# A transformer layer with compressive memory: copying projections out of PSUM in pairs, masks by two heads, tiles at a pitch of 130, another warm-up and another order

## The chip, the cores and the metric

The kernel runs on one core of one Trainium2 chip. The metric is the device time of one execution in microseconds (us). A core has five engines with a queue each: PE (TensorE, the matmuls; its weight loads are shown as PEld), DVE (VectorE), ACT (ScalarE), POOL (GpSimd) and SP (SyncE, which issues nearly all DMAs here). An engine takes its instructions in the order of its queue and stops at one whose semaphore has not come yet.

## The reference

The input x has 2048 rows of 576 columns. Everything is bfloat16 in memory.

```python
h  = x + attention(layernorm(x), wq, wk, wv, wo, beta)       # 32 heads of 18 columns
h2 = h + (gelu(layernorm(h) @ w1 + b1) @ w2 + b2)            # w1: 576 x 4608, w2: 4608 x 576

# attention, for each of 4 segments of 512 rows
p     = softmax(q_s @ k_s.T * 18**-0.5 + causal mask)
o     = g * (phi(q_s) @ M) / (phi(q_s) @ z + 1e-6) + (1 - g) * (p @ v_s)    # g = sigmoid(beta)
M, z  = M + phi(k_s).T @ v_s, z + sum(phi(k_s))              # phi(t) = t + 1 above 0, exp(t) below
```

For segment 0 the memory M is zero, so only the softmax part counts there; all later segments read a memory that the earlier ones have filled.

## The kernel before, in words

**The order is written out.** The kernel first builds a list of operations (`add`). Each has a tag of its stage, a name, a function that issues its instructions, the operations it comes behind (`after`), the buffers it acquires (`acq`) and uses. The table `TIMETABLE` gives each an engine and a slot: `"B00Po": "p 264"` puts that projection on PE in slot 264; the letters are p (PE), a (ACT), d (DVE), g (POOL) and s (SP). All operations are issued in the order of their slots, so this table is the order of every engine's queue. The costs that stand beside the operations choose which buffer of a set an operation gets; the order does not depend on them.

**Stages.** X is the first layernorm: of each tile of 128 rows DVE sums (`stats`, L752), POOL forms the reciprocal deviation (`rstd`, L769 and L770), and DVE writes the normalized tile `xn` in bfloat16 (`apply`, L782; L780 for the first two, which only subtract the mean, the deviation being put into the copies of the projections behind them). `xn` is then turned: for X0 and the first two tiles of X1 by PE transposes out of a tile with 640 columns in one run (`transposes`, L790, copied out of PSUM by `copy`), for the others through DRAM by a transposing DMA (`flip`, L665).

P projects q, k and v. `proj_pair` (L843) computes a tile's 576 output columns as two halves of 288, each in a PSUM bank of its own. It is two operations, P and R. If they stand next to each other in PE's queue they are issued as ten matmuls over 128 rows (L875); if another operation stands between them they are issued as 18 matmuls over 64 rows each (L849), and a small memset (`pass`, L855) on DVE or POOL lies between the two. Each half was copied out of PSUM by an operation of its own (`copy`, L669 to L680: ACT at L675, DVE at L679, with a factor L673 and L677) into `qk_pad` (q and k, 32 columns for each head) or `v_aug`. `qk_pad` goes to DRAM and comes back turned by flips; the flips of segment 1 are called `A1flip`. From k also come `pk` and `fk` (L955), which with v make the memory update M (L979, L991).

A0 is the attention of segment 0, in `step` (L1044): scores on PE (`st0`, L1060) for four heads at a time, two activations exp on ACT, each over 1024 columns of PSUM (L1009), then the causal mask on the blocks of the diagonal: one operation for all four heads and two blocks, 128 x 1024 (on DVE a product with a triangle, L1072; on POOL an affine select, L1075). It came behind both exponentials. Then values on PE (L1091), a 32x32 transposition on DVE (`valT`, L1105), reciprocals (`rec`, L1109 and L1110), the division (`comb`, L1114, DVE or POOL), a copy of two leftover columns per head (`swap`), and five transpositions on DVE per pair of row tiles into `oT` (L1130); those of the first pair are called `A01oT`. A1 to A3 do the same for the later segments, with the memory (scores L1220, masks L1232 and L1234, values L1245, memory L1191 and L1194).

B is the output projection, by the same `proj_pair` (so `B00Po` is the first half of that of segment 0's first tile), the residual and the second layernorm (`apply`, L782 again). C is the first matmul of the MLP (F1: L1394 for segment 0, L1357 for the others), copied out with b1 (L1405, L1372, L1370, L1362) and put through gelu (L1377, L1411). D is the second one (F2, L1446), with the residual (L1459).

**The start.** PE warms up on a tile `pt` that DVE first sets to zero (L683), in three operations of 4, 3 and 2 matmuls (L689). A gate (`gate_x`, L739) copies one element of x on DVE once x has landed; the DMAs of some weights and of more x are held until then (`held`, L727). The list `begin` holds back later fills and loads in the same manner: `ones`, two activations on ACT that set a column of `v_aug` to one, and on POOL the fills of the blocks of the memory (`memset`, `eps`, `gmz`).

Of the kernel before, what the change touches and what calls it, by code (L numbers as in the profile page):

```python
# [25 lines left out]
    "A00exp": "a 93 103 111 128",  # L26
    "A00mask": "g 162 132 182 179",
    "A00st0": "p 90 110",
    "A01comb": "d189 g198 d236 g240",
    "A01exp": "a 148 151 160 164 180 184 171 173",  # L30
    "A01mask": "g169 d158 g193 g194",
    "A01oT": "d 209 244 253 252 261",
    "A01rec": "d 177 192 226 224",
    "A01st0": "p 140 159 178 166",
    "A01swap": "g 256 251",
    "A01val": "p 172 218",
    "A01valT": "d 176 175 223 219",
    "A02comb": "g 407 430",
    "A02exp": "a 210 213 242 243 225 228 263 270 282 292 314 317 339 345",
    "A02mask": "g 238 260 298 362",  # L40
    "A02rec": "d 376 410",
    "A02st0": "p 197 234 216 258 280 304 335",
    "A02val": "p 302 303 371 372",
    "A02valT": "d 311 379",
    "A03comb": "g 483 498",
    "A03exp": "a 365 366 403 408 374 375 412 413 417 418 439 449 452 465",
    "A03mask": "g 414 388 423 470",
    "A03oT": "d 445 460 516 519 543",
    "A03rec": "d 442 493",
    "A03st0": "p 364 386 373 405 416 429 451",  # L50
    "A03swap": "g 525 532",
    "A03val": "p 434 438 489 490",
    "A03valT": "d 441 491",
    "A0flip": "s 89 86 141 117 183 188 259 348",
    "A1comb": "g622 g683 g750 g788 d834 g866 g905 g907",
    "A1comb2": "d641 g692 d772 g804 g847 d870 g935 d910",
    "A1eg": "a 436 428 617 702 548 768 746 817",
    "A1exp": "a 499 500 515 518 510 512 614 616 588 589 627 628 649 650 666 669 691 693 710 713 734 737 779 781 754 756 801 806 810 815 790 792 848 859 "
        "869 874 877 882 831 832",
    "A1flip": "s 421 420 572 631 478 695 662 807",  # L60
    "A1mask": "g554 d546 g556 g559 g542 g644 g621 g600 d655 g667 g694 g703 g718 g730 g742 d749 d755 g791 d793 d796 g819 g814 g844 g822 g794 d872 g862 g891 "
        "g880 g894 g890 g856",
    "A1mem": "p 530 454 682 761 709 849 811 878",
    "A1memT": "d 531 455 688 773 719 851 813 879",
    "A1memfin": "g607 g533 g766 g789 g777 g861 d919 g900",
    "A1oT": "d 823 873 871 936 937",
    "A1pq": "d 511 440 677 748 698 836 799 867",
    "A1rec": "d 561 464 745 780 765 852 840 881",
    "A1rec2": "d 599 663 733 775 828 858 902 904",
    "A1rg": "g 501 425 584 696 604 743 770 830",  # L70
    "A1st": "p 494 514 509 606 586 624 647 665 679 704 726 764 740 800 805 787 843 854 876 825",
    "A1swap": "d911 g920",
    "A1val": "p 590 648 708 763 808 846 892 895",
    "A1valT": "d 591 653 712 774 816 853 898 901",
    "A2comb": "d1034 d1078 g1154 g1120 g1166 d1192 g1289 g1275",
    "A2comb2": "g1070 d1081 d1222 g1145 d1167 g1217 g1292 d1283",
    "A2eg": "a 889 930 1097 1058 1012 1136 1171 1210",
    "A2exp": "a 917 918 893 896 924 925 908 914 940 942 1032 1044 1045 1051 1027 1030 1064 1068 1073 1074 1104 1106 1092 1100 1126 1129 1112 1117 1132 "
        "1137 1159 1160 1176 1178 1227 1234 1184 1188 1202 1204",
    "A2flip": "s 786 845 916 984 969 1080 928 1182",  # L80
    "A2mask": "d985 g1006 d987 d977 g965 g956 g962 g966 d1057 d1076 g1079 d1047 g1052 g1077 g1089 d1088 g1115 d1107 d1118 d1139 g1142 g1158 g1170 d1162 "
        "g1211 d1228 g1220 d1241 g1235 g1206 d1209 d1225",
    "A2mem": "p 931 1009 1147 1084 1127 1177 1239 1240",
    "A2memT": "d 941 1028 1148 1095 1140 1185 1247 1246",
    "A2memfin": "g976 g1053 d1216 g1122 d1163 d1195 g1274 g1269",
    "A2oT": "d 1111 1264 1244 1299 1303",
    "A2pq": "d 906 979 1099 1067 1024 1153 1197 1226",
    "A2rec": "d 975 1042 1190 1121 1150 1191 1254 1266",
    "A2rec2": "d 1023 1066 1119 1113 1157 1186 1265 1271",
    "A2rg": "g 860 951 1046 1060 1005 1133 1172 1189",  # L90
    "A2st": "p 915 888 923 903 939 1031 1040 1007 1056 1069 1101 1083 1124 1109 1130 1144 1165 1223 1183 1201",
    "A2swap": "g 1297 1293",
    "A2val": "p 1014 1013 1085 1090 1146 1179 1243 1242",
    "A2valT": "d 1017 1018 1093 1096 1149 1180 1255 1250",
    "A3comb": "g1389 g1417 g1468 d1513 d1563 g1585 g1653 d1633",
    "A3comb2": "d1431 g1432 g1523 d1548 d1645 g1594 g1662 d1636",
    "A3eg": "a 1280 1298 1394 1388 1516 1478 1550 1564",
    "A3exp": "a 1272 1273 1281 1288 1290 1296 1390 1391 1306 1307 1436 1437 1409 1415 1398 1399 1445 1450 1426 1428 1518 1526 1462 1466 1480 1481 1528 "
        "1531 1501 1504 1557 1560 1593 1603 1605 1607 1567 1569 1576 1577",
    "A3flip": "s 1238 1214 1302 1286 1333 1439 1421 1458",  # L100
    "A3mask": "d1309 g1304 d1329 g1338 g1359 d1396 g1347 d1314 d1446 d1418 d1425 g1444 g1435 d1454 d1449 g1443 d1532 g1472 g1474 g1537 g1514 d1536 g1509 "
        "g1525 d1590 g1626 g1604 d1608 g1621 g1572 d1588 d1602",
    "A3mem": "p 1381 1352 1471 1463 1541 1533 1616 1617",
    "A3memT": "d 1387 1353 1494 1491 1553 1534 1644 1618",
    "A3memfin": "g1419 g1393 d1496 g1510 d1638 d1551 g1660 g1631",
    "A3oT": "d 1498 1624 1659 1665 1667",
    "A3pq": "d 1313 1342 1401 1448 1527 1493 1582 1584",
    "A3rec": "d 1412 1368 1495 1497 1580 1535 1654 1623",
    "A3rec2": "d 1357 1416 1464 1507 1562 1559 1646 1630",
    "A3rg": "g 1301 1215 1375 1354 1512 1490 1482 1545",  # L110
    "A3st": "p 1262 1278 1287 1380 1305 1429 1406 1397 1442 1413 1508 1457 1477 1524 1500 1543 1589 1601 1561 1573",
    "A3swap": "a1661 g1656",
    "A3val": "p 1346 1402 1459 1465 1546 1544 1628 1627",
    "A3valT": "d 1348 1414 1461 1469 1549 1547 1641 1629",
    "B00Po": "p 264",
    "B00Ro": "p 272",
    "B00T": "p 336 340",
    "B00apply": "d 315",
    "B00copy": "d 338 341",
    "B00dma": "s 232 540",  # L120
    "B00hadd": "d 279 281",
    "B00pass": "d 266",
    "B00rstd": "g 312",
    "B00stats": "d 309",
    "B00tail": "g 326",
    "B01Po": "p 274",
    "B01Ro": "p 278",
    "B01T": "p 343 346",
    "B01apply": "d 325",
    "B01copy": "d 344 347",  # L130
    "B01dma": "s 235 447",
    "B01hadd": "d 283 294",
    "B01pass": "d 275",
# [12 lines left out]
    "B03Po": "p 610",
    "B03Ro": "p 612",
    "B03apply": "d 656",
    "B03dma": "s 549 769 678",
    "B03flip": "s 776 778",  # L150
    "B03hadd": "d 613 615",
    "B03pass": "d 611",
    "B03rstd": "g 654",
    "B03stats": "d 635",
    "B03tail": "d 660",
    "B1Po": "p 944 959 961 947",
    "B1Ro": "p 949 970 971 950",
# [345 lines left out]
def kernel(  # L503
# [12 lines left out]
    P = 128  # L516
# [1092 lines left out]
```

## Time and profile before

| | us |
|---|---|
| median of 3 runs | 442.07 (442.07 to 442.28) |
| the profiled execution | 442.22 |
| its span, first to last instruction | 440.5 |
| PE busy | 431.3 of it (98%), 5152 matmuls |
| DVE, ACT, POOL busy | 289.6, 300.0, 179.7 |
| moved by DMA | 75.61 MB |

The profile is one execution. A row of a group reads: line, engine, operation, written tile <- read tile with partitions x elements, count | busy us, mean ns of one | idle time of the engine just ahead of them, and the releaser that ended most of it. A row of the chain or of the timeline reads: start in us from the span's start, length, then engine, tile and line, and in brackets the idle time ahead of it. A row of a window reads: stretch, length, busy us (and instructions) of PE, PEld, DVE, ACT and POOL, the granted TensorE clock, the mean share of the DMA engines and GB/s. The granted clock was 1.000 of full speed in the whole span.

### The profile page before, as it was taken

Reading aid. Unit: us, or ns where it says so; the run is one execution under the profiler, and the core shown is the slowest. Engines: PE = TensorE matmul, PEld = TensorE weight load, DVE = VectorE, ACT = ScalarE, POOL = GpSimd, SP = SyncE. Lnnn points to the kernel's source line nnn. Section 1 sums busy time; section 2 is a strip of 40 time slices with the busy share of each in tenths; the row PEclk is TensorE's granted clock in tenths of the full one; section 3 lists DMA queues with packets and bytes.
Section 4 is the critical chain, followed back from the end, with each engine's and each line's share of the span. In section 5 each row is a group of like instructions: output and inputs, shape, how many; then the busy total and the mean of one; then the engine's idle time right before and its main releaser. Section 6 shows DMA issues by size and latency. Waiting matters only on the chain.

```text
span 440.5 us, 12357 instructions
## 1 busy us (share of the span) xinstructions
PE 431.3 (98%) x5152; PEld 278.7 (63%) x5152; DVE 289.6 (66%) x650; ACT 300.0 (68%) x344; POOL 179.7 (41%) x327
## 2 busy tenths in 40 slices
PE   8997999999999999999999999999999999999997
PEld 4764677766677676663445766644457775446885
DVE  5899999998889869749797877784957101000111
ACT  5998789999988888786989966556974001755000
POOL 4698676757557454445223643512304100000001
PEclk9999999999999999999999999999999999999999
DMA  7789899989989782683752376506440490650020
GB/s 218 255 182 286 240 243 330 257 243 263 206 268 376 184 220 89 156 231 81 254 141 59 124 220 171 151 13 218 132 132 25 120 235 11 214 167 1 28 94 28
DMA packets 80279, 75.61 MB, mean 172 GB/s; under 512 B 57952, under 2 KB 67424, under 8 KB 80224
## 3 DMA queue, kind: packets, MB, share of 16 engines
q1 hardware_dynamic: 80080, 74.74, 61.7%
q8 instruction: 40, 0.66, 0.6%
q14 instruction: 15, 0.12, 0.1%
q10 hardware_dynamic: 144, 0.09, 0.1%
HBM read 42.30 MB, written 18.87 MB: 139 GB/s over the span
## 4 chain that ended last, share of the span: by engine, by line
PE 86%; DVE 6%; DMA 5%; ACT 1%; issue 1%; SPq 0%; DVEq 0%
PE bank L1446 33%; PE bank L1357 24%; PE bank L849 8%; PE bank L1394 6%; PE bank L875 5%; PE bank L1220 4%; PE bank L1245 3%; DMA qk<-qkd 2%; DMA hT<-in_A_w_dram 1%; DMA qkd<-qk_pad 1%; PE bank L1194 1%; DVE t L1105 1%; PE bank L1191 1%; DMA x<-in_A_x_dram 1%; DVE xn L782 1%
## 5 line engine op out<-in xcount | busy, mean ns | idle before, releaser
L1009 ACT ACTIVATE pt<-bank 128x1024 bf16<-128x1024 f32 x160 | 155.6, 1023 | 37.1 <-PE bank L1220 19.3
L1446 PEld LDWEIGHTS <-hT 128*128 128x128 bf16 x1188 | 111.5, 98 | 32.8 <-issue 5.9
L1357 PE MATMUL bank<-xreg,w1g 64*128 64x512 bf16 x972 | 108.2, 376 | 0.0
L1357 PEld LDWEIGHTS <-w1g 64*128 64x128 bf16 x972 | 46.1, 94 | 56.5 <-issue 3.4
L1446 PE MATMUL bank<-w,hT 128*128 128x288 bf16 (+2 forms) x594 | 78.0, 283 | 0.0
L1446 PE MATMUL bank<-w_lo,hT 128*128 128x288 bf16 (+2 forms) x594 | 77.4, 283 | 0.0
L1234 POOL TENSOR_SCALAR_AFFINE_SELECT pt<-pt 128x512 bf16<-128x512 bf16 x59 | 41.3, 711 | 43.3 <-ACT pt L1009 42.9
L1459 DVE TENSOR_TENSOR ot<-bank,hc 128x288 bf16<-128x288 f32 (+2 forms) x33 | 14.2, 444 | 62.4 <-PE bank L1446 60.0
L1362 ACT ACTIVATE hT<-bank,b_col 128x512 bf16<-128x512 f32 x36 | 22.1, 689 | 46.4 <-PE bank L1357 46.2
L1432 POOL TENSOR_TENSOR hc<-hc,b_bc 128x576 f32<-128x576 f32 x8 | 10.2, 1279 | 87.1 <-DVE hc L1432 81.9
L1372 DVE TENSOR_SCALAR hT<-bank,b_col 128x512 bf16<-128x512 f32 x46 | 32.8, 739 | 14.4 <-PE bank L1357 11.8
L1394 PE MATMUL bank<-xreg,w1g 64*128 64x256 bf16 x648 | 38.4, 269 | 0.1
L875 PE MATMUL bank<-hT,xreg 128*128 128x288 bf16 x250 | 33.9, 286 | 1.8 <-DVE qk_pad L679 1.6
L1394 PEld LDWEIGHTS <-w1g 64*128 64x128 bf16 x648 | 30.9, 94 | 6.4 <-issue 2.9
L1377 ACT ACTIVATE hT<-hT 128x8192 bf16<-128x8192 bf16 (+2 forms) x6 | 31.8, 5319 | 0.1
L875 PEld LDWEIGHTS <-xreg 128*128 128x128 bf16 x250 | 23.5, 98 | 9.5 <-issue 3.1
L1432 DVE TENSOR_TENSOR hc<-hc,b_bc 128x576 f32<-128x576 f32 x8 | 6.0, 747 | 27.5 <-DMA hc<-hd 27.5
L1232 DVE TENSOR_TENSOR pt<-pt,tri 128x512 bf16<-128x512 bf16 x37 | 19.3, 533 | 7.1 <-ACT pt L1009 7.1
L1220 PE MATMUL bank<-qk 32*128 32x512 bf16 (+3 forms) x384 | 23.8, 301 | 0.0
L849 PE MATMUL bank<-hT,xreg 64*128 64x288 bf16 x342 | 23.1, 283 | 0.1
L1370 ACT ACTIVATE hT<-bank,b_col 128x512 bf16<-128x512 f32 x26 | 17.0, 690 | 8.3 <-PE bank L1357 8.1
L1184 DVE SCALAR_TENSOR_TENSOR e<-e,r 128x512 bf16<-128x512 bf16 x24 | 19.1, 798 | 3.2 <-POOL r L1182 1.8
(122 smaller groups left out, 588.4 us busy)
## 6 DMA issues: line engine op xcount, KB each, us to landing
w1g<-in_B_w_dram SPq DMA_DIRECT2D x41, 576.0 KB, 4.5
qkd<-qk_pad SPq DMA_DIRECT2D x15, 512.0 KB, 3.5
hd<-h SPq DMA_DIRECT2D x16, 288.0 KB, 3.9
hc<-hd SPq DMA_DIRECT2D x16, 288.0 KB, 3.4
w_lo<-in_B_w_dram SPq DMA_DIRECT2D x3, 864.0 KB, 5.9
w<-in_B_w_dram SPq DMA_DIRECT2D x3, 864.0 KB, 10.2
xb<-in_A_x_dram SPq DMA_DIRECT2D x16, 144.0 KB, 3.9
x2d<-xn SPq DMA_DIRECT2D x14, 160.0 KB, 2.7
```

Of the source, the lines that this page charges most:

```text
L849: return nc.tensor.matmul(out=cc[hf].t[:, 0:HALF], lhsT=xTb.t[r, k, ts], rhs=wt[r, hf, k, :], start=start, stop=stop, skip_group_check=True)
L875: nc.tensor.matmul(out=cc[hf].t[:, 0:HALF], lhsT=xTb.t[:, k, ts], rhs=wt[:, hf, k, :], start=(k == 0), stop=(k == KT - 1))
L1009: ops.append(add(prio, {"act": 1.04}, lambda e, j=j: nc.scalar.activation(out=pt.t[:, 2 * j:2 * j + 2, :], in_=st[j].t[:], func=ACT.Exp, s ...
L1220: nc.tensor.matmul(out=st[i // 2].t[:, i % 2, off:off + n_], lhsT=qk[rows, 1, kt * P:(kt + 1) * P], rhs=qk[rows, 0, kt * P:L], start=True, ...
L1232: nc.vector.tensor_tensor(out=blk, in0=blk, in1=tri[:].unsqueeze(1).to_broadcast([P, 4, P]), op=ALU.mult)
L1234: nc.gpsimd.affine_select(out=blk, in_=blk, pattern=[[0, 4], [1, P]], compare_op=ALU.is_ge, fill=0.0, base=0, channel_multiplier=-1)
L1357: nc.tensor.matmul(out=cc[w].t[:], lhsT=w1.t[rows, k, q, :], rhs=x2T[s].t[rows, k, :], start=(k == 0), stop=(k == ND - 1))
L1362: ready_f[f + w] = [add(pf - 12, {"act": 0.68}, lambda e, f=f, w=w, cc=cc: nc.scalar.activation(out=hT[:, :, f + w, :], in_=cc[w].t[:].rea ...
L1372: nc.vector.tensor_scalar(out=dst, in0=src, scalar1=b, scalar2=None, op0=ALU.add)
L1377: ge = add(2.9, {"act": 0.42 * (f1 - f0) + 0.2}, lambda e, f0=f0, f1=f1: nc.scalar.activation(out=hT[:, :, f0:f1, :], in_=hT[:, :, f0:f1, ...
L1394: nc.tensor.matmul(out=cc[w].t[:, q * 2 * P:(q + 1) * 2 * P], lhsT=w1.t[rows, k, q, :], rhs=x2T[s].t[rows, k, ts], start=(k == 0), stop=(k ...
L1446: nc.tensor.matmul(out=c.t[:, 0:c1 - c0], lhsT=hT[:, tl // 2, f, (tl % 2) * P:(tl % 2 + 1) * P], rhs=w2_c[ch][:, f - ch * WCH, c0:c1], sta ...
```

## The change

- **Pairs.** The two halves of q, k or v get one PSUM buffer of two neighbouring banks, and one copy moves both: 44 copies where there were 88.
- **Masks of segment 0.** One mask becomes two, by two heads each (128 x 512), and each comes behind its own exponential: 32 where there were 16. On DVE there are 6 where there was 1, on POOL 26 where there were 15.
- **Pitch.** Tiles of `xn` are five runs of 128 columns at a pitch of 130 where PE transposes them (six writes: the four tiles of X0 and two of X1), on the writing and on the reading side.
- **Warm-up.** It reads a constant that is there before the kernel starts; the memset goes. It is 4, 4 and 2 matmuls.
- **`begin`.** `ones` and POOL's fills of the memory blocks no longer come behind it. `ones` goes from slots 233 and 377 to 31 and 18.
- **Smaller ones.** The gate goes from DVE to POOL; the copy of b1 (L679 before, 128 x 36, on DVE) is an operation of its own name; costs of `rec` and `b1` are told to the planner; a loop over `KEEP` is added, and `KEEP` is empty.
- **A new timetable**, nearly every slot of it, 1909 operations where there were 1938.

```diff
@@ timetable, some rows
-    "A00mask": "g 162 132 182 179",
+    "A00mask": "g141 d152 g157 g121 g175 g170 g173 d163",
-    "A01comb": "d189 g198 d236 g240",
+    "A01comb": "g210 g216 d233 d232",
-    "A01mask": "g169 d158 g193 g194",
+    "A01mask": "d158 g169 d166 g167 g191 g196 d189 d200",
-    "A01oT": "d 209 244 253 252 261",
+    "A01oT": "d 214 230 255 254 259",
-    "A02st0": "p 197 234 216 258 280 304 335",
+    "A02st0": "p 205 271 218 239 285 316 332",
-    "A1flip": "s 421 420 572 631 478 695 662 807",
+    "A1flip": "s 449 405 534 607 496 636 667 788",
-    "B00Po": "p 264",
+    "B00Po": "p 268",
-    "P1copy": "a214 d215 a239 d229 d359 a361 d167 d168 d199 d200 a250 a254 a323 d333 a331 d334 a308 a307 a267 d271 a295 a296 d399 d393",
+    "P1copy": "a227 a267 a351 d171 a202 a237 a327 d338 a299 d260 a306 d388",
-    "P1fk": "d 299 217 383 354",
+    "P1fk": "d 331 265 394 362",
-    "warm": "p 5 19 23",
+    "warm": "p 0 2 17",
@@ build
-        warm_ok = add(-9.5, {"dve": 0.25}, lambda e: nc.vector.memset(warm[:], 0.0), name="memset")
-        wprev = warm_up(4, 1.72, [warm_ok], [Buf(c_s), Buf(c_s)])
-        wprev = warm_up(3, 1.29, [wprev], [Buf(c_s), Buf(c_s)])
+        wprev = warm_up(4, 1.72, [], [Buf(c_s), Buf(c_s)])
+        wprev = warm_up(4, 1.72, [wprev], [Buf(c_s), Buf(c_s)])
@@ layernorm, apply
+                if gaps:
+                    dst, srcs = dst_buf.t[:].rearrange("p (k c) -> p k c", c=PITCH)[:, :, 0:P], src().rearrange("p (k c) -> p k c", c=P)
@@ stage_P
-                    cc = [Buf(c_s), Buf(c_s)]
-                    for hf, c in enumerate(cc):
-                        evs[nm, hf] = copy(p0 - 0.5, 0.41, 0.46, lambda hf=hf, n=n, pad=pad: pad.t[:, hf * 4:(hf + 1) * 4, n, :, 0:Dh],
+                    c = Buf(c_s, width=2)
+                    evs[nm, 0] = copy(p0 - 0.5, 0.66, 0.76, lambda n=n, pad=pad: pad.t[:, :, n, :, 0:Dh].rearrange("p (h g) i d -> p h g i d", h=2),
+                    evs[nm, 1] = evs[nm, 0]
@@ stage_A0, step
-                for u in range(0, len(diag), 2):
+                for u, j in ((u, j) for u in range(0, len(diag), 2) for j in range(2)):
-                        blk = pt.t[:, :, o0:o0 + 2 * w].rearrange("p i (b q) -> p i b q", q=w)[:, :, :, 0:P]
+                        blk = pt.t[:, 2 * j:2 * j + 2, o0:o0 + 2 * w].rearrange("p i (b q) -> p i b q", q=w)[:, :, :, 0:P]
-                    masks[u] = add(ps, {"dve": 0.87, "pool": 1.17}, mask, [*ex, tri_ok], None, [pt], name="mask")
+                    masks[u, j] = add(ps, {"dve": 0.45, "pool": 0.67}, mask, [ex[j], tri_ok], None, [pt], name="mask")
```

More of the change, by code (lines that the diff above doesn't have):

```diff
@@ L624, in to_w2 @@
             w2_c.extend(late.tile([P, WCH, D], BF16, name=f"w2_{c}") for c in range(3, NF // WCH))
-    warm = pt_s.tiles[0][:, 0, :]
+    warm = nc.const_aps.tensor(1.0, (P, 512), BF16)
     banks_all = psum.tile([P, 8, 512], F32, name="bank")
@@ L843, in proj_pair, with half @@
         def proj_pair(prio, xTb, tl, nm, after, cc):
+            own = cc if isinstance(cc, list) else [cc]
+            def half(hf):
+                return cc[hf].t[:, 0:HALF] if isinstance(cc, list) else cc.t[:, hf, 0:HALF]
             ts = slice(tl * P, (tl + 1) * P)
@@ L848, in rows @@
                 r = slice(64 * w, 64 * w + 64)
-                return nc.tensor.matmul(out=cc[hf].t[:, 0:HALF], lhsT=xTb.t[r, k, ts], rhs=wt[r, hf, k, :], start=start, stop=stop, skip_group_check=True)
+                return nc.tensor.matmul(out=half(hf), lhsT=xTb.t[r, k, ts], rhs=wt[r, hf, k, :], start=start, stop=stop, skip_group_check=True)
             last, passed = [], []
@@ L874, in fn_b @@
                     for k in range(KT):
-                        nc.tensor.matmul(out=cc[hf].t[:, 0:HALF], lhsT=xTb.t[:, k, ts], rhs=wt[:, hf, k, :], start=(k == 0), stop=(k == KT - 1))
-            a = add(prio, {"pe": 0.613}, fn_a, list(after) + w_ok[nm], cc, [xTb], table="rows64", name="P" + nm)
+                        nc.tensor.matmul(out=half(hf), lhsT=xTb.t[:, k, ts], rhs=wt[:, hf, k, :], start=(k == 0), stop=(k == KT - 1))
+            a = add(prio, {"pe": 0.613}, fn_a, list(after) + w_ok[nm], own, [xTb], table="rows64", name="P" + nm)
             f = add(prio, {"dve": 0.07, "pool": 0.13}, fn_f, [a], name="pass")
-            b = add(prio, {"pe": 0.49}, fn_b, [a, f], None, cc + [xTb], table="rows64", name="R" + nm)
+            b = add(prio, {"pe": 0.49}, fn_b, [a, f], None, own + [xTb], table="rows64", name="R" + nm)
             a.mate, f.fence = b, a
@@ L1515, in build @@
         later.append(gates[0])
-        mz_gates = [add(3.55, {"pool": 0.31}, lambda e, i=i: gmz_fn(i), begin + [gates[0]], name="gmz") for i in range(4)]
+        mz_gates = [add(3.55, {"pool": 0.31}, lambda e, i=i: gmz_fn(i), [gates[0]], name="gmz") for i in range(4)]
         w_ok["o"] = load_w(4, "o", 3, begin)
@@ L1538, in build @@
             stage_C(s, 20.0 + s)
+        gr.tag = "K"
+        for first, n, then, m, count in KEEP:
+            a = [o for o in gr.ops if o.tag + o.name == first][n]
+            b = [o for o in gr.ops if o.tag + o.name == then][m]
+            c = Buf(c_s)
+            k = add(50, {"pe": 0.056 * count}, lambda e, c=c, count=count: [nc.tensor.matmul(
+                out=c.t[:, 0:P], lhsT=ident[:], rhs=ident[:], start=True, stop=True) for _ in range(count)], [a, ident_ok], c, name="keep")
+            b.after.append(k)
         return gr
```

66 lines of the change are left out of this document (34 added, 32 removed), and 611 rows, old and new, of the table TIMETABLE.

## The prediction, made before the changed kernel was run

> **What bounds the kernel now.** I read the page first, then the busy time in stretches of ten microseconds, then the chain that ended last. The page's first block:
>
> ```profile
> PE 431.3 (98%) x5152; PEld 278.7 (63%) x5152; DVE 289.6 (66%) x650; ACT 300.0 (68%) x344; POOL 179.7 (41%) x327
> ```
>
> TensorE is busy for 98% of a span of 440.5 us. The profiled execution took 442.22 us, 1.7 us more than its span; the median of the runs is 442.07. Busy is not yet useful, so the next question is where the missing 2% lies:
>
> ```profile
> 0.00:10.00 10.00, 7.86 (x45) 4.29 (x46) 5.49 (x19) 6.55 (x13) 4.78 (x16) 1.00 0.69 206
> 10.00:20.00 10.00, 9.90 (x119) 7.54 (x118) 8.28 (x23) 8.51 (x16) 5.26 (x11) 1.00 0.77 266
> 20.00:30.00 10.00, 9.28 (x170) 6.88 (x169) 9.33 (x24) 10.00 (x15) 9.32 (x14) 1.00 0.84 189
> 30.00:40.00 10.00, 8.73 (x156) 6.33 (x156) 9.79 (x23) 8.65 (x12) 8.05 (x12) 1.00 1.05 283
> 40.00:50.00 10.00, 8.58 (x105) 5.27 (x102) 9.92 (x24) 7.22 (x13) 6.58 (x15) 1.00 0.73 205
> 50.00:60.00 10.00, 10.00 (x186) 7.31 (x184) 9.80 (x25) 8.87 (x12) 8.74 (x32) 1.00 1.12 258
> ```
>
> The columns after the length are PE, PEld, DVE, ACT, POOL. Up to 50 us PE idles 2.14, 0.10, 0.72, 1.27 and 1.42 us, together 5.65. Of the 9.2 us that 431.3 leaves of the span, 3.1 more lie behind the last matmul stream (401.88 + 35.49 = 437.4, next fence), so the 387 us between lose only some 0.4. In 30 to 50 us DVE is busy 19.71 of 20: there the vector engine sets the pace. The chain says the same:
>
> ```profile
> 23.69 0.49 DVE xreg L679
> ...
> 42.42 1.00 DVE oT L1130 x3
> ...
> 45.91 0.40 PE bank L1060 x7
> ...
> 366.81 35.07 PE bank L1357 x324
> 401.88 35.49 PE bank L1446 x324
> ```
>
> From 23.69 to 45.91 us it runs through DVE's queue; after that nearly all of it is matmul, and the last two rows are streams without a gap. So a new order gains in two ways only: TensorE gets fewer or cheaper matmuls, or the DVE queue that holds it back up to 46 us ends sooner. The reader is to keep one point of that queue: the last transposition of `A01oT`, which ends at 42.42 + 1.00 = 43.42 us. The output projection of the first row tile (B00) stands behind it on PE, and the waits of PE show it:
>
> ```profile
> PE bank L875 <- DVE qk_pad L679: 1.6, 2, 1.2
> PE bank L875 <- DVE oT L1130: 1.0, 1, 1.0
> ```
>
> **The change, part by part: TensorE.** I sorted both timetables by engine. The matmuls are the same but for three things. One 512-column matmul is added to the warm-up. Of 60 pairs P/R of projections, 28 were adjacent and ran as ten 128-row matmuls; now 24 are, so four more run as 18 half-row ones. The list changes its tiling (128, 64 or 32 rows, 32 columns) 193 times where it was 191.
>
> ```profile
> 16.63 2.56 PE bank L875 x20
> ...
> 106.47 2.31 PE bank L849 x36
> ...
> 126.90 2.07 PE bank L1394 x36
> ...
> 157.53 1.97 PE bank L1394 x36
> ```
>
> Two adjacent pairs take 2.56 us, two split ones 2.31: four more split ones save 4 x 0.125 = 0.5 us. The same 36 matmuls take 2.07 us with a change of tiling behind them and 1.97 without: 0.10 us each, so two more cost 0.2. **PE's sum: -0.3 us.** Of the lists up to B00's first projection, one operation differs: `A02st0` 1, eight matmuls, stood ahead of it and now stands behind; at the rate of the chain's row at 45.91 (seven in 0.40) that is 0.46 us at most. Behind the wait for `A01oT` PE's work is therefore 0 to 0.16 longer, and I take 0: the end moves as that wait does.
>
> **The start.** The warm-up no longer waits for a memset, so it can start earlier, and it is a matmul longer:
>
> ```profile
> 1.24 3.17 PE L689 MATMUL bank<-pt 128*128 128x512 bf16 x7 [1.24 <-DVE pt L683]
> ...
> 9.35 2.61 PE L888 MATMUL bank<-hT,xreg 128*128 128x288 bf16 x20 [0.52 <-DMA hT<-in_A_w_dram]
> ```
>
> I cost it at nothing: what hides it is the wait for the weights of q, which ends at 9.35 us by a DMA. SyncE issues the first ten DMAs in the same order as before. PE idles 0.52 us ahead of that weight, so the two fills of `ones` on ACT (now between the first reductions and the second copy of x) and the POOL fills released from `begin` have that much cover. Without it `ones` would cost up to two activations, estimated at 0.6 each from the 738 ns of a larger one below: 0 to +0.7 us, kept for the range. Likewise the gate goes from DVE to POOL: DVE loses one small cast, the held DMAs wait for the same piece of x.
>
> **DVE's queue up to 29.9 us**, the end of the statistics of X2's first tile, in both tables with nearly the same work around it:
>
> ```profile
> L782 DVE TENSOR_SCALAR xn<-x,ln 128x640 bf16<-128x640 bf16 x6 | 3.8, 635 | 1.4 <-POOL ln L770 1.4
> ...
> L679 DVE CAST qk_pad<-bank 128x288 bf16<-128x288 f32 x4 | 1.7, 448 | 0.1
> ...
> L679 DVE CAST v_aug<-bank 128x288 bf16<-128x288 f32 x3 | 1.4, 451 | 0.0
> L677 DVE TENSOR_SCALAR v_aug<-bank,ln 128x288 bf16<-128x288 f32 x2 | 0.9, 504 | 0.0
> ...
> L780 DVE TENSOR_SCALAR xn<-x,mean_b 128x640 bf16<-128x640 bf16 x2 | 0.8, 388 | 0.1
> L1072 DVE TENSOR_TENSOR pt<-pt,tri 128x1024 bf16<-128x1024 bf16 x1 | 0.7, 725 | 0.0
> ```
>
> and, over the whole span, what the new shapes are nearest to:
>
> ```profile
> L1234 POOL TENSOR_SCALAR_AFFINE_SELECT pt<-pt 128x512 bf16<-128x512 bf16 x59 | 41.3, 711 | 43.3 <-ACT pt L1009 42.9
> ...
> L1405 DVE TENSOR_TENSOR hT<-bank,b_col 128x512 bf16<-128x512 f32 x31 | 20.2, 671 | 0.9 <-PE bank L1394 0.8
> ...
> L1232 DVE TENSOR_TENSOR pt<-pt,tri 128x512 bf16<-128x512 bf16 x37 | 19.3, 533 | 7.1 <-ACT pt L1009 7.1
> ...
> L1075 POOL TENSOR_SCALAR_AFFINE_SELECT pt<-pt 128x1024 bf16<-128x1024 bf16 x15 | 18.1, 1211 | 3.0 <-ACT pt L1009 2.8
> ...
> L675 ACT CAST qk_pad<-bank 128x288 bf16<-128x288 f32 x21 | 8.5, 427 | 1.4 <-ACT pt L1009 0.4 <-PE bank L875 0.3 <-PE bank L849 0.3
> ...
> L673 ACT ACTIVATE qk_pad<-bank,ln 128x576 bf16<-128x576 f32 x4 | 2.8, 738 | 0.4 <-PE bank L888 0.2 <-POOL ln L770 0.2
> ```
>
> A pair on ACT costs 738 ns for two halves of 427: 0.12 saved. On DVE the trace has no such shape. Above: two halves, 0.90. Below: the 671 ns of 512 columns. Carrying the step from 288 to 512 columns on by 64 gives 0.74, which I take. Nine halves (4.1 us) stood in this stretch; four pairs (3.0) and one copy of 1024 transposed columns (1.1, with the ACT copies of that shape as its neighbours) stand there now: **0**. Masks: one of 0.73 becomes four of 0.53: **+1.4**. POOL's 15 large ones (1211 ns each) become 26 small (711): 0.3 us more, on the emptier engine.
>
> The six tiles written at a pitch of 130: their six writes took 0.39 twice (L780) and, of L782, all but two; these four include the waits shown next.
>
> ```profile
> 9.49 0.84 POOL L655 MEMSET qk_pad<- 128x896 bf16 x1
> 9.58 0.94 DVE L782 TENSOR_SCALAR xn<-x,ln 128x640 bf16<-128x640 bf16 x1 [1.00 <-POOL ln L770]
> ```
>
> The same form takes 388 ns when nothing is in its way, and 0.94 here, begun under a POOL instruction and ended 0.19 behind it: POOL held something DVE needed. The pitched form lies between 0.39 (unchanged, and at best free of waits) and 0.72 (the slowdown as large as a mask of 1024 columns); I take 0.55. Six of these are 3.3 us against 2 x 0.39 + 3.8 - 1.3 (the two plain ones) = 3.3: **0**, with -1.0 to +1.0 as bounds. [...]
>
> Against the +1.4 stand the 1.4 us that this queue idled for POOL's rstd (L782's row), which ready work can fill, since each mask now waits for one exponential. I take most of that, and this stretch as **+0.1**; with none of it filled it would be +1.4.
>
> **DVE's queue from 29.9 us to the last oT:**
>
> ```profile
> L679 DVE CAST qk_pad<-bank 128x288 bf16<-128x288 f32 x4 | 1.7, 438 | 0.0
> L1114 DVE TENSOR_TENSOR o_nat<-t,r 128x288 bf16<-128x288 f32 x2 | 1.7, 836 | 0.0
> L679 DVE CAST b_col<-ot 128x36 f32<-128x36 bf16 x1 | 1.1, 1078 | 0.0
> ...
> L955 DVE SCALAR_TENSOR_TENSOR fk_pad<-ek,rk 128x576 bf16<-128x576 bf16 x1 | 0.7, 737 | 0.0
> ```
>
> The new table puts behind the oT what stood ahead of it: four halves of P1's copies (1.7 less their overlap of 0.3), `fk` (0.7), the copy of b1 (1.1). Into it go two masks (1.1), a `swap` and X2's first `apply` (0.4 each, by L780). Two `comb` stay on DVE and two on POOL, but it is those of the other row tile that DVE does now: the last one in its way (0.84) goes to POOL. The sum is -3.2 - 0.8 + 1.9 = -2.1; the added ones are of the kind that waits for POOL, for which I put back 0.5 (two to three of them as long as the mask of 0.73 instead of 0.53). **-1.6.** What moved behind is then late: the P1 copies, `fk` and b1 must be done in the time PE takes for B00, B01 and the next scores; where they aren't, each microsecond comes back, as DVE stays above 9.8 of 10 until 60 us. ACT gains 0.1 us per pair and gets no more than before ahead of its exponentials.
>
> **Sum:** +0.1 - 1.6 + 0 = -1.5 us on 442.07: **440.6 us.**
>
> **Rivals.** (a) **The wait only moves**: masks and the late copies hold PE at the next scores and DVE's total, 0.4 us apart in the two tables, decides. Then PE's -0.3 and what noise there is are left: 441.8. For it: DVE is full until 60 us. Against: PE needs DVE's work in the order that the chain shows, and that order is what changed. (b) **More goes**: the waits for POOL go almost entirely (the 0.5 put back, the 1.0 of the pitched writes) and the 0.4 behind 50 us too: 440.6 - 0.5 - 1.0 - 0.4 = 438.7. (c) **Slower, by a late transposed load:** `A1flip` 0 moves in SyncE's queue from directly behind flip 1 to behind two loads of w1, a store and two small ones.
>
> ```profile
> 61.44 8.11 DMA qk<-qkd
> ```
>
> ```profile
> 79.47 0.39 PE L1220 MATMUL bank<-qk 32*128 32x512 bf16 x4
> ```
>
> It took 8.11 us, and its first reader, `A1st0` 0, came ten later. In the new table PE has about 5 us of matmuls between the flip's place and that reader: an F1 (2.07), two projections (2.31), a memory update. Issued there it would hold PE for 3.1 us: 440.6 + 3.1 = 443.7. It decides from the point at which SyncE issues the flip less than 8.1 us ahead of the reader. Against: what SyncE waits for there is the buffer of the w1 load, freed three F1 (6.2), two projections (2.3) and the update ahead of the reader, so 8.5 us and more. (d) The pitch doing nothing is inside the bounds of the write above: no separate time.
>
> **How the numbers follow.** A measurement of this kernel can tell about 0.2% (0.9 us) from no change; faster is below 441.2, slower above 443.0. My forecast, 439.4 to 441.2: 0.39. (b), below that: 0.18. (a), 441.2 to 443.0: 0.18. (c) and other late transfers in a wholly new queue, above 443.0: 0.25. So faster 0.57, same 0.18, slower 0.25. The range leaves 0.08 below and 0.12 above: 437.0 to 444.6; its lower end is (b) with another 1.5 us of early idle time gone, its upper (c) with 0.9 us from `ones` and waits.
>
> **What would show it.** Right: the last L1130 of the first tile ends near 41.9 us; split pairs at L849 number 648 matmuls, L875 240; PE is full from 50 us on; the pitched writes near 0.55 us and none near 0.94. Wrong: oT still beyond 43 us (the ledger of DVE is missed), or a PE gap behind 60 us that a DMA ends (c), or one behind L679 in 42 to 55 us (a). The prediction also fails if the start misses its cover, which shows as q's first matmul later than 9.4 us.

## The result and the profile after

The changed kernel takes 440.17 us (median of 8 runs, 438.78 to 441.30) against 442.07 us (8 runs, 441.11 to 442.73): a ratio of 0.9958, with a 95% interval of 0.9945 to 0.9970, so 1.9 us or 0.4% faster. The forecast was 440.6 us. Its profiled execution took 441.04 us with a span of 439.3; that is one of its longer ones, and a second profile, below, shows why.

The page's first block, changed kernel:

```profile
PE 431.0 (98%) x5182; PEld 279.0 (64%) x5182; DVE 288.5 (66%) x641; ACT 298.2 (68%) x325; POOL 176.5 (40%) x328
```

The stretches of ten microseconds (columns after the length: PE, PEld, DVE, ACT, POOL):

```profile
0.00:10.00 10.00, 8.81 (x51) 5.00 (x52) 5.98 (x19) 6.37 (x12) 6.22 (x21) 1.00 0.72 215
10.00:20.00 10.00, 9.20 (x101) 7.10 (x99) 8.33 (x22) 8.51 (x16) 6.27 (x17) 1.00 0.70 250
20.00:30.00 10.00, 9.05 (x182) 6.62 (x180) 9.43 (x19) 9.83 (x12) 8.42 (x15) 1.00 0.82 182
30.00:40.00 10.00, 7.92 (x155) 5.46 (x142) 9.58 (x30) 8.71 (x12) 6.87 (x19) 1.00 1.18 180
40.00:50.00 10.00, 9.93 (x169) 6.68 (x171) 7.58 (x21) 8.05 (x11) 7.52 (x22) 1.00 1.09 326
50.00:60.00 10.00, 9.72 (x182) 7.41 (x180) 9.30 (x22) 8.67 (x12) 7.37 (x19) 1.00 1.00 319
```

From 40 to 50 us PE now idles 0.07 us where it idled 1.42, and DVE is busy for 7.58 where it was for 9.92: there it no longer sets the pace. From 30 to 40 us PE idles 2.08 where it idled 1.27. The chain that ended last and the list of PE's waits name the cause:

```profile
30.90 9.12 DMA xreg<-xnd
40.07 2.99 PE bank L859 x46
```

```profile
PE bank L859 <- DMA xreg<-xnd: 1.7, 1, 1.7
```

`xreg<-xnd` is X1's flip, the transposing load of the third and fourth row tile of segment 1. It takes 9.12 us, and PE, which has come to its reader early, waits 1.7 us for it. Before, PE waited 1.0 us for `A01oT` and 1.6 us for DVE's copies of q and k; the first is not in the list any more, and of the second 0.3 us is left.

### The profile page after: what moved, and what is told of

Same layout as the page of the kernel before. It is cut to its first block, busy times and chain, and to the rows that moved or that the text cites. A ratio compares the mean times of both kernels' runs of the same rounds, so it can differ in the third digit from the quotient of the medians.

```text
span 439.3 us, 12412 instructions
## 1 busy us (share of the span) xinstructions
PE 431.0 (98%) x5182; PEld 279.0 (64%) x5182; DVE 288.5 (66%) x641; ACT 298.2 (68%) x325; POOL 176.5 (40%) x328
## 4 chain that ended last, share of the span: by engine, by line
PE 89%; DMA 4%; DVE 3%; SPq 1%; POOL 1%; ACT 1%; issue 1%; DVEq 0%; POOLq 0%
PE bank L1453 33%; PE bank L1364 24%; PE bank L859 9%; PE bank L1401 8%; PE bank L1227 4%; PE bank L885 3%; PE bank L1252 3%; DMA xreg<-xnd 2%; DMA x<-in_A_x_dram 2%; PE bank L1201 1%; PE bank L1098 1%; PE bank L1067 1%; SPq L663 1%; SPq L670 1%; PE bank L1198 1%
## 5 line engine op out<-in xcount | busy, mean ns | idle before, releaser
L1241 POOL TENSOR_SCALAR_AFFINE_SELECT pt<-pt 128x512 bf16<-128x512 bf16 x57 | 38.0, 680 | 45.4 <-ACT pt L1016 45.1
L1439 POOL TENSOR_TENSOR hc<-hc,b_bc 128x576 f32<-128x576 f32 x11 | 14.5, 1333 | 83.6 <-DMA hc<-hd 83.6
L1401 PE MATMUL bank<-xreg,w1g 64*128 64x256 bf16 x648 | 38.4, 270 | 0.0
L859 PE MATMUL bank<-hT,xreg 64*128 64x288 bf16 x414 | 27.7, 283 | 1.7 <-DMA xreg<-xnd 1.7
L885 PE MATMUL bank<-hT,xreg 128*128 128x288 bf16 x210 | 28.4, 287 | 0.3 <-ACT pt L1016 0.2
L1412 DVE TENSOR_TENSOR hT<-bank,b_col 128x512 bf16<-128x512 f32 x33 | 21.4, 681 | 6.3 <-PE bank L1401 5.9
L859 PEld LDWEIGHTS <-xreg 64*128 64x128 bf16 x414 | 19.6, 94 | 8.3 <-DMA xreg<-xnd 1.9
L885 PEld LDWEIGHTS <-xreg 128*128 128x128 bf16 x210 | 19.7, 98 | 6.4 <-issue 1.0
L773 POOL TENSOR_TENSOR ln<-ln,mhalf 128x1 f32<-128x1 f32 x32 | 19.5, 610 | 2.7
```

The costliest lines, as they stand in the source:

```text
L859: return nc.tensor.matmul(out=half(hf), lhsT=xTb.t[r, k, ts], rhs=wt[r, hf, k, :], start=start, stop=stop, skip_group_check=True)
L885: nc.tensor.matmul(out=half(hf), lhsT=xTb.t[:, k, ts], rhs=wt[:, hf, k, :], start=(k == 0), stop=(k == KT - 1))
L1241: nc.gpsimd.affine_select(out=blk, in_=blk, pattern=[[0, 4], [1, P]], compare_op=ALU.is_ge, fill=0.0, base=0, channel_multiplier=-1)
L1401: nc.tensor.matmul(out=cc[w].t[:, q * 2 * P:(q + 1) * 2 * P], lhsT=w1.t[rows, k, q, :], rhs=x2T[s].t[rows, k, ts], start=(k == 0), stop=(k ...
L1412: nc.vector.tensor_tensor(out=dst, in0=src, in1=b.unsqueeze(2).to_broadcast([P, 2, 2 * P]), op=ALU.add)
```

## The experiments

Each is set against runs of the kernel before on the same chip (medians 441.81 to 442.25 us). The changed kernel's own ratio was 0.9958 (0.9945 to 0.9970).

**The order alone, and the operations alone.** The first keeps the new timetable and takes the operations back; the second does the reverse, except that the projections of segments 2 and 3 keep their halves.

```diff
@@ e1_order_alone, against the changed kernel
-    PITCH = 130
+    PITCH = 128
...
-    warm = nc.const_aps.tensor(1.0, (P, 512), BF16)
+    warm = pt_s.tiles[0][:, 0, :]
...
+                for h in range(parts):
+                    to, frm = (dst()[:, h], src()[:, h]) if parts > 1 else (dst(), src())
...
+                        nc.scalar.copy(out=to, in_=frm)
...
-                        blk = pt.t[:, 2 * j:2 * j + 2, o0:o0 + 2 * w].rearrange("p i (b q) -> p i b q", q=w)[:, :, :, 0:P]
...
+                        blk = pt.t[:, :, o0:o0 + 2 * w].rearrange("p i (b q) -> p i b q", q=w)[:, :, :, 0:P]
...
@@ e2_operations_alone, against the changed kernel
...
-    "P1copy": "a227 a267 a351 d171 a202 a237 a327 d338 a299 d260 a306 d388",
...
+    "P1copy": "d215 a239 a361 d168 d200 a254 d333 d334 a308 d271 a296 d399",
...
```

> The new order with the old operations: each pair of halves is two copies of 288 columns one behind the other on the pair's engine, masks of segment 0 by four heads at the later of the two slots, xn in one run of 640 columns, warm-up of 4+3+2 matmuls behind a memset. Theory O (the order of DVE's queue ahead of A01oT brings the gain, the operations themselves nearly nothing): 440.0 to 440.8 us, 1.3 to 2.0 below before. Rival C (cheaper copies and masks bring it): 441.6 us or more.

> The old order with the new operations: pairs for the projections of segments 0 and 1 at the later half's slot and engine (halves stay for segments 2 and 3, where the old order has no two neighbouring banks free), masks by two heads one behind the other, pitch 130, constant for the warm-up, ones at its old place. Theory O: 441.5 to 442.6 us, no gain to speak of. Rival C: 440.2 to 440.8 us, most of the gain.

The order alone gave 440.82 us, a ratio of 0.9968 (0.9956 to 0.9980): 1.3 us faster than the kernel before. The operations alone gave 442.76 us, 1.0009 (1.0000 to 1.0018): no gain, if anything a loss. Rival C falls in both. Theory O fits better, though both medians lie a little above its ranges (440.82 against 440.8, 442.76 against 442.6). The gain comes with the order. What the operations add once the order is there, 0.9968 against 0.9958, is not told apart from nothing: these two intervals overlap. On DVE their part can be seen. The transpositions of `A01oT`, first with the order alone and then with the operations alone (shortest, median and longest in ns, then the first and the last start in us):

```profile
L1144 DVE STREAM_TRANSPOSE oT<-o_nat x5: 402/439/447, 36.5 to 41.3; 128x256 bf16<-128x256 bf16 x5
```

```profile
L1144 DVE STREAM_TRANSPOSE oT<-o_nat x5: 391/397/436, 36.4 to 42.5; 128x256 bf16<-128x256 bf16 x5
```

The last one starts at 41.3 and 42.5 us. In the kernel before it started at 43.0, and with both changes it starts at 40.1 where nothing else holds it (second profile, below). So the order takes 1.7 us out of this queue by itself, the operations 0.5, and both together 2.9.

**Each operation taken back by itself, in the new order.**

```diff
@@ e4_pitch_128
-    PITCH = 130
+    PITCH = 128
...
@@ e5_memset_warm
-    warm = nc.const_aps.tensor(1.0, (P, 512), BF16)
+    warm = pt_s.tiles[0][:, 0, :]
...
+                if not after:
+                    nc.vector.memset(warm[:], 0.0)
...
-        wprev = warm_up(4, 1.72, [wprev], [Buf(c_s), Buf(c_s)])
+        wprev = warm_up(3, 1.29, [wprev], [Buf(c_s), Buf(c_s)])
@@ e6_halves
...
+                for h in range(parts):
+                    to, frm = (dst()[:, h], src()[:, h]) if parts > 1 else (dst(), src())
...
+                        nc.scalar.copy(out=to, in_=frm)
...
@@ e11_big_masks
...
-                        blk = pt.t[:, 2 * j:2 * j + 2, o0:o0 + 2 * w].rearrange("p i (b q) -> p i b q", q=w)[:, :, :, 0:P]
...
+                        blk = pt.t[:, :, o0:o0 + 2 * w].rearrange("p i (b q) -> p i b q", q=w)[:, :, :, 0:P]
...
```

> The changed kernel with xn in one run of 640 columns again (pitch 128), the order unchanged. [...]

> The changed kernel with the old warm-up only: a memset of pt on DVE and 4+3+2 matmuls behind it. Theory S (the start hides it: PE waits for q's weights anyway): within 0.3 us of 440.2, and q's weights land early or late whatever the warm-up reads. Rival W (the constant is what makes q's weights come without a wait, as in four runs with it, against two with the memset that waited 0.5 and 1.3 us): 0.5 to 1.2 us slower than 440.2, with a wait of PE for the weights of q near 8.5 to 10 us.

> The changed kernel with each pair of halves copied by two instructions of 288 columns one behind the other, in the same place and on the same engine. Theory O: a pair on DVE is 0.15 us longer, on ACT 0.21; three of DVE's and about ten of ACT's pairs stand ahead of the output projection, and ACT has idle time there: 440.2 to 440.8. Rival C: 441.2 us or more.

> The changed kernel with masks of segment 0 by four heads, at the later of the two slots and on its engine (14 on POOL, 2 on DVE, 128 x 1024), behind both exponentials. Theory O: values wait up to 0.3 us longer here and there, DVE has 1.8 us less to do: 440.0 to 440.8. Rival C: 441.2 us or more.

| | us | ratio to before | interval |
|---|---|---|---|
| pitch 128 (12 runs, 439.18 to 443.02) | 440.87 | 0.9972 | 0.9956 to 0.9989 |
| warm-up behind a memset (10 runs) | 440.14 | 0.9959 | 0.9945 to 0.9974 |
| halves one by one (8 runs) | 440.36 | 0.9966 | 0.9953 to 0.9978 |
| masks by four heads (12 runs) | 440.35 | 0.9966 | 0.9953 to 0.9979 |

None is told apart from the changed kernel. The medians of e5, e6 and e11 lie in the ranges of S and O, and rivals C (441.2 and more) fall. The runs of e4 do not decide what the pitch is worth: 440.87 is 0.7 us above the changed kernel's 440.17, and the interval, some 440.1 to 441.6 us, holds no loss as well as one of 1.4. W's lower end (0.5 us) lies inside e5's interval, so a loss of that size is not excluded, but W's mechanism is: PE waited for q's weights with the constant too, 0.8 us in the profile of e9 below.

The pitch is best seen in the writes themselves. The six of the changed kernel, and then those of pitch 128, in order of time on DVE:

```profile
4.07 0.55 DVE L786 TENSOR_SCALAR xn<-x,mean_b 128x640 bf16<-128x640 bf16 x1
...
5.33 0.55 DVE L786 TENSOR_SCALAR xn<-x,mean_b 128x640 bf16<-128x640 bf16 x1
...
9.96 0.61 DVE L788 TENSOR_SCALAR xn<-x,ln 128x640 bf16<-128x640 bf16 x1
...
13.99 0.60 DVE L788 TENSOR_SCALAR xn<-x,ln 128x640 bf16<-128x640 bf16 x1 [0.46 <-POOL ln L773]
...
17.39 0.60 DVE L788 TENSOR_SCALAR xn<-x,ln 128x640 bf16<-128x640 bf16 x1
...
22.30 0.55 DVE L788 TENSOR_SCALAR xn<-x,ln 128x640 bf16<-128x640 bf16 x1
```

```profile
4.05 0.46 DVE L786 TENSOR_SCALAR xn<-x,mean_b 128x640 bf16<-128x640 bf16 x1
...
5.23 0.65 DVE L786 TENSOR_SCALAR xn<-x,mean_b 128x640 bf16<-128x640 bf16 x1
...
9.97 0.98 DVE L788 TENSOR_SCALAR xn<-x,ln 128x640 bf16<-128x640 bf16 x1
...
13.98 0.79 DVE L788 TENSOR_SCALAR xn<-x,ln 128x640 bf16<-128x640 bf16 x1 [0.46 <-POOL ln L773]
...
17.56 0.44 DVE L788 TENSOR_SCALAR xn<-x,ln 128x640 bf16<-128x640 bf16 x1
...
22.48 0.40 DVE L788 TENSOR_SCALAR xn<-x,ln 128x640 bf16<-128x640 bf16 x1
```

As one run of 640 columns a write takes 0.40 to 0.98 us; at a pitch all six take 0.55 to 0.61. The third one, begun beside the same POOL memset in both kernels (9.92 to 10.76 us), takes 0.98 us as one run and 0.61 at the pitch. The six sum to 3.46 us at the pitch and 3.72 without it.

**X1's flip, and what is late behind it.**

```diff
@@ e3_flip_ahead
-    "X1flip": "s 198",
+    "X1flip": "s 194.5",
@@ e7_x_behind_residual: e3 and
-    "X3dma": "s 209 447 451 398 537 546",
+    "X3dma": "s 246 447 451 398 537 546",
@@ e8_residual_first: e3 and
-    "B00dma": "s 240 443",
-    "B01dma": "s 245 639",
+    "B00dma": "s 196 443",
+    "B01dma": "s 197 639",
...
-                          [combs[s][5] if s else combs[0, tl]], acq=xb)
+                          [combs[s][5]] if s else [], acq=xb)
@@ e9_stats_later: e7 and
-    "X2stats": "d 178 187 302 343",
+    "X2stats": "d 178 187 317 343",
@@ e12_rstd_later: e9 and
-    "X2rstd": "g 199 241 328 367",
+    "X2rstd": "g 199 241 331 367",
```

> The changed kernel once more, unaltered, for a second profile of it. If the landing of X1's transposing load sets its time: about 441.0 where the load takes 9.1 us, about 439.2 to 440.0 where it takes 7.0 to 7.7, and PE's wait for it 1.7 us or none. If it does not: the same time whatever the load took.

> The changed kernel, and X1's transposing load is issued ahead of the load of wo instead of behind it (slot 194.5 for 198 in SyncE's queue), nothing else. Theory F (the 1.7 us for which PE waits at 40.07 for that load is the last thing that is late there; DVE would be done with A01oT at about 40.4): 438.7 to 439.5 us, PE's wait for it under 0.7 us. Rival Q (DVE's queue or the load of wo takes over at once): 440.0 to 440.5 us, the wait goes to another tile.

> As e3_flip_ahead, and the load of X3's first rows goes behind the two loads of residual rows xb (slot 246 for 209 in SyncE's queue). In e3 the residual add waited 2.2 us for xb, which took 6.5 us to land, and PE waited 1.0 us for that add. Theory F2 (that wait is what ate the gain of e3): the wait gets shorter by 0.6 us and more, 439.4 to 439.9 us. Rival N (landing times at this place are what they are, whatever the queue): 440.2, as e3.

> As e3_flip_ahead, and the two loads of residual rows xb are issued directly behind the load of wo (slots 196 and 197 for 240 and 245), without coming behind the first division. Theory F2: no wait of the residual add for xb, none of PE behind it: 438.7 to 439.6 us. Rival N: 440.2 us, another load (X1's transposing one, or w_lo) is later by as much.

> As e7_x_behind_residual, and the sums of X2's third tile go in DVE's queue behind the transposition, the copy of b1 and the first apply of B00 (slot 317 for 302). In e7 DVE stood 1.25 us for that tile's rows of x, and PE waited 0.92 us for the transposition behind it. Theory F2 (each wait that goes lets the next one show until the DMA behind it is moved too): 438.7 to 439.3 us. Rival N: 439.9, as e7.

> As e9_stats_later, and the reciprocal deviation of X2's third tile goes in POOL's queue behind the tail copy of B01 (slot 331 for 328). In e9 POOL took 1.4 us for it ahead of that copy, and PE waited 0.8 us for the copy. Theory F2: that wait goes, 439.0 to 439.4 us, the best of these orders. Rival N (each wait that goes is taken up by the next one): 439.6 to 440.0, as e9.

The changed kernel again: 439.99 us (6 runs), 0.9950 (0.9936 to 0.9963). In this second profile the flip landed in 7.3 us, and PE waited 0.20 us ahead of its reader instead of 1.7:

```profile
DMA to landing us min/median/max: 7.3/7.3/7.3
```

```profile
38.57 2.38 PE L859 MATMUL bank<-hT,xreg 64*128 64x288 bf16 x36 [0.20 <-DMA xreg<-xnd]
```

This execution took 439.65 us, the one with 9.12 us took 441.04: the 1.4 us between them are about the 1.5 us by which the two waits differ, as was expected. With pitch 128 the flip landed in 7.0 us (439.18), in e6 in 7.6 (439.88), in e5 in 9.1 (441.60, of which 0.6 was a wait for weights). It is not the only landing that counts: e1's profile took 441.36 us with 7.7, of which 1.3 was a wait for weights, and e12's took 441.06 us with the flip landing in 3.9; there PE waited 1.3 us for a copy of q or k on ACT, and from 10 to 20 us it was busy for 8.40 us against 9.68 in the changed kernel's second profile. That the flip spreads the runs without a profile as well is likely, not shown.

Issued ahead of the load of wo, the flip took 5.7 us to land in e3, 5.3 in e7, 5.8 in e8, 5.2 in e9 and 3.9 in e12, and PE waited for it in none of them. But e3 is no faster for that: 440.20 us, 0.9954 (0.9941 to 0.9967). Theory F as it was put (438.7 to 439.5) falls, and rival Q holds (440.0 to 440.5, the wait goes to another tile). Which tile, e3's profile shows, in the list of PE's waits and DVE's timeline:

```profile
PE bank L1067 <- DVE h L1304: 1.0, 1, 1.0
```

```profile
43.59 0.82 DVE L1304 TENSOR_TENSOR h<-bank,xb 128x288 f32<-128x288 f32 x2 [2.18 <-DMA xb<-in_A_x_dram]
```

PE comes to the flip's reader, and with it to B00, 2.4 us earlier than in the changed kernel's first profile, and now the residual rows `xb` are late: the add waits 2.18 us, holds its PSUM bank, and the next scores wait 1.0 us. With the rows of X3 behind `xb` (e7: 439.88 us, 0.9956, 0.9944 to 0.9968) that wait is gone, and the next one shows:

```profile
PE bank L859 <- DVE t L1112: 0.9, 1, 0.9
```

```profile
47.37 0.82 DVE L757 BATCH_NORM_STATS2 ln<-x 128x6 f32<-128x288 bf16 x2 [1.25 <-DMA x<-in_A_x_dram]
...
48.35 0.67 DVE L1112 STREAM_TRANSPOSE t<-bank 128x512 f32<-128x512 f32 x1
```

DVE stands 1.25 us at sums whose rows have not landed, and the transposition behind them, which PE needs, is late. In e8 (440.50 us, 0.9968, 0.9957 to 0.9979; a miss) this same wait was 0.8 us, and its profile lost time at the start as well. With these sums moved back (e9: 439.77 us, 0.9946, 0.9933 to 0.9959) it is POOL's turn:

```profile
PE bank L802 <- POOL xn L1309: 0.8, 1, 0.8
PE bank L898 <- DMA hT<-in_A_w_dram: 0.8, 1, 0.8
```

With POOL's `rstd` of that tile moved back too (e12) the runs gave 439.49 us (5 runs, 438.83 to 441.06), 0.9936 (0.9922 to 0.9949): the best of all, and faster than the kernel before by 2.7 us. Against the changed kernel's 0.9958 and 0.9950 the intervals still touch. Each step's median moved by less than the wait that it removed: 0.3, 0.1 and 0.3 us (e7, e9, e12) for 1.0, 0.9 and 0.8. By the ranges that were expected, e7 lies at the edge of F2's, e8 and e9 lie on N's side, and e12 between the two; the intervals of neighbouring steps overlap, so no single step is shown to gain.

## Why the prediction was right, and where its steps were off

**The bound.** Right: the queue of DVE ahead of `A01oT` held PE, and its order brought the gain (e1 against e2). Rival (a), that the wait only moves within DVE, falls with it: from 40 to 50 us DVE is busy 7.58 of 10.

**PE's sum.** The -0.3 us is too small for the profiles to confirm: the page's sums are 431.3 and 431.0, but 431.8 in the second profile of the same changed kernel. The counts are as named, 414 + 234 = 648 matmuls in split pairs and 210 + 30 = 240 in adjacent ones:

```profile
L859 PE MATMUL bank<-hT,xreg 64*128 64x288 bf16 x414 | 27.7, 283 | 1.7 <-DMA xreg<-xnd 1.7
L885 PE MATMUL bank<-hT,xreg 128*128 128x288 bf16 x210 | 28.4, 287 | 0.3 <-ACT pt L1016 0.2
...
L859 PE MATMUL bank<-wt_o,oT 64*128 64x288 bf16 x234 | 15.7, 283 | 0.0
...
L885 PE MATMUL bank<-wt_o,oT 128*128 128x288 bf16 x30 | 4.2, 287 | 0.0
```

**The start at nothing.** The size is right within what the runs can tell (e5), but the cover was not the one named. Before, PE stood 0.52 us for the weights of q; in both profiles of the changed kernel it did not. In the first of them the forty matmuls of the first projections, q's among them, ran on as one group:

```profile
6.22 5.06 PE L898 MATMUL bank<-hT,xreg 128*128 128x288 bf16 x40
```

In e9, with the same start, the weights came late again (0.8 us).

**The new shapes.** Groups of the whole span, changed kernel:

```profile
L683 DVE CAST qk_pad<-bank 128x576 bf16<-128x576 f32 x17 | 12.7, 751 | 1.4 <-PE bank L859 1.1 <-issue 0.2
...
L679 ACT CAST qk_pad<-bank 128x576 bf16<-128x576 f32 x11 | 7.1, 645 | 2.6 <-PE bank L859 1.3 <-PE bank L885 0.8 <-POOL ln L773 0.3
...
L1079 DVE TENSOR_TENSOR pt<-pt,tri 128x512 bf16<-128x512 bf16 x6 | 3.2, 549 | 0.0
```

A pair on DVE takes 751 ns (forecast 0.74 us; with a factor for each row, L681, some 810), a mask 549 on the mean (533). A pair on ACT takes 645 where the row of a scaled copy had given 738: the saving per pair is 0.21 us, not 0.12. The pitched write at 0.55 was right as well: the six took 0.55 to 0.61 us, against 0.40 to 0.98 without the pitch (e4). Beside the POOL memset the write of one run took 0.98 us and the pitched one 0.61; what makes the difference was not shown.

**DVE's queue up to the last oT: mis-sized in both stretches.** The forecast had it end at 41.9 us. The last transposition ran here in the changed kernel, first and second profile:

```profile
41.59 0.45 DVE L1137 STREAM_TRANSPOSE oT<-o_nat 128x256 bf16<-128x256 bf16 x1
```

```profile
40.09 0.45 DVE L1137 STREAM_TRANSPOSE oT<-o_nat 128x256 bf16<-128x256 bf16 x1
```

The first, 42.04 us, looks like the forecast but is not the queue's own end: the `pass` ahead of it stood 1.60 us for PE, which stood for the flip. In the second profile, without that wait, the queue ends at 40.54 us, 2.9 us earlier than before and not 1.5. The statistics of X2's first tile, which part the two stretches, end there at 30.65 us, where they ended at 29.9:

```profile
30.44 0.21 DVE L758 BATCH_NORM_AGGREGATE ln<-ln 128x2 f32<-128x12 f32 x1
```

So the first stretch is 0.7 us longer, not 0.1, and the second 3.6 us shorter, not 1.6. In the first, the four masks took 609 ns each where 533 was forecast, and of the 1.4 us of idle time for rstd 0.5 stayed. Up to 30 us, and then from 29.9 to 43.42 us (changed kernel):

```profile
L1079 DVE TENSOR_TENSOR pt<-pt,tri 128x512 bf16<-128x512 bf16 x4 | 2.4, 609 | 0.0
```

```profile
L1079 DVE TENSOR_TENSOR pt<-pt,tri 128x512 bf16<-128x512 bf16 x2 | 0.9, 430 | 0.0
```

In the second stretch the two masks took 430 ns each: the 0.5 us put back for waits for POOL, the author's estimate, was not needed. Rows got shorter there, as rival (b) had it, but they are rows that it did not price. The kernel before and the changed one from 29.9 to 43.42 us:

```profile
L1110 DVE TENSOR_TENSOR r<-r,omg_q 128x16 f32<-128x16 f32 x4 | 2.2, 545 | 0.1
```

```profile
L1121 DVE TENSOR_TENSOR o_nat<-t,r 128x288 bf16<-128x288 f32 x2 | 0.8, 426 | 0.0
L1117 DVE TENSOR_TENSOR r<-r,omg_q 128x16 f32<-128x16 f32 x4 | 0.7, 184 | 0.2
```

One term came out by luck. The prediction took off 0.8 us because a `comb` would go to POOL; two `comb` stand ahead of the last oT on DVE now as before. The 0.8 us came all the same, because they take 426 ns each instead of 836. Before, one of the two took 1.23 us, from 32.09 us on, and lay within POOL's two masks (31.91 to 34.28 us); the other took 0.44.

Four products of 16 columns took 545 ns each and take 184: 1.4 us that the prediction had left out of its sum. Together with the 0.5 put back, and less the 0.6 that the first stretch lost beyond the forecast, that makes, within 0.1 us, the 1.4 by which the forecast was short. Before, each of the four ended 0.02 or 0.03 us behind a POOL instruction that ran beside it; the longest ended at 34.30 us, 0.02 behind the second of two masks (34.28):

```profile
31.91 2.37 POOL L1075 TENSOR_SCALAR_AFFINE_SELECT pt<-pt 128x1024 bf16<-128x1024 bf16 x2 [0.15 <-ACT pt L1009]
```

```profile
33.51 0.79 DVE L1110 TENSOR_TENSOR r<-r,omg_q 128x16 f32<-128x16 f32 x1
```

Beside those POOL instructions the products took 545 ns on the mean, and 184 in the changed kernel; why they take longer there was not shown. Not every neighbour counts: in the changed kernel a product at 33.44 us took 0.17 us inside POOL's rstd of one column (33.33 to 33.90 us).

Is it the small masks or the order? With the old order and small masks (e2) they still take 538 ns, with the new order and large masks (e11) 337:

```profile
L1124 DVE TENSOR_TENSOR r<-r,omg_q 128x16 f32<-128x16 f32 x4 | 2.2, 538 | 0.1
```

```profile
L1120 DVE TENSOR_TENSOR r<-r,omg_q 128x16 f32<-128x16 f32 x4 | 1.3, 337 | 0.2
```

So the order is the larger part (0.8 us of the 1.4), and the small masks add the rest only inside it.

**What is late next.** The prediction looked for it in the late P1 copies (a) and in `A1flip` 0 (c). Neither showed: PE's list of waits holds none for the transposed load `qk<-qkd`, and none for L683 above 0.3 us. It was X1's flip, which the working never followed because its place in SyncE's queue hardly changed (30.99 and 30.90 us): what changed was its reader, to which PE came at about 39.6 us before and now at 38.4. Rival (c) had the right mechanism at the wrong transfer, and its price here was 1.7 us or less, out of a larger gain. That the sum came within 0.4 us of the measured time is luck: two errors of opposite sign, 1.4 us of gain not seen on DVE and up to 1.7 us of loss not seen at a DMA, about cancel.

**PE full from 50 us on.** Nearly: it idles 0.28 us from 50 to 60.

**The tail** was taken as unchanged and is not. The last store is issued 0.3 us behind PE's last matmul (437.35 and 436.62 us) in both kernels, but the span ends 2.83 us behind it before and 2.36 us now (440.5 - 437.67, 439.3 - 436.94):

```profile
437.67 0.33 SPq L659 DMA_DIRECT2D out_dram<-ot  x1
```

```profile
436.94 0.33 SPq L663 DMA_DIRECT2D out_dram<-ot  x1
```

The changed kernel's second profile ends this way too (2.38 us), and e2, with the old order, ends like the kernel before (437.72 to 440.5). Some 0.5 of the 1.9 us are thus outside the stretch that the prediction was about; what takes the time there was not traced.

## What to carry to other kernels

When the queue that holds the longest engine gets shorter, list the inputs of everything that this engine reads in the next few microseconds, and compare each one's landing time with the new moment of need: a transfer that has not moved becomes late because its reader has (here X1's flip, by 1.7 us in one profile and 0.20 in the other). Some DVE instructions here took much longer than their like and ended 0.02 to 0.04 us behind one of POOL (545 ns on the mean against 184, 1.08 us against 0.14): compare each with the shortest of the same form, look whether it ends with an instruction of POOL, and count the difference as time that may go when that neighbour moves. Here each change of order gained less than the wait that it removed (0.3, 0.1 and 0.3 us for 1.0, 0.9 and 0.8); set the next waits in a row before counting it.

## What the runs showed of the hardware that was not expected

A copy of 128 x 36 on DVE (b1) took 1.08 us before, and its end, 42.42 us, lies 0.04 us behind that of the POOL mask beside it. In the changed kernel, at another place, it takes 0.14 us. Before, POOL first and then DVE:

```profile
41.28 1.10 POOL L1075 TENSOR_SCALAR_AFFINE_SELECT pt<-pt 128x1024 bf16<-128x1024 bf16 x1
```

```profile
41.34 1.08 DVE L679 CAST b_col<-ot 128x36 f32<-128x36 bf16 x1
```

And one and the same transposing load took 7.3 and 9.1 us to land in two executions of one kernel (7.0 to 9.1 in all seven profiles with this place in the queue), and 3.9 to 5.8 us in five others in which it was issued ahead of the load of wo instead of behind it.
